# Two forward blocks ahead of the first backward block in the opening of a gated FFT and MLP gradient kernel

## The chip, the cores and the metric

The kernel runs on one core of one Trainium2 chip. The metric is the time of one execution on the device in microseconds (us). Before the change, three runs had a median of 1196.28 us (1195.99 to 1197.32). All other times come from one profiled execution of the same kernel. In its views PE is TensorE, DVE is VectorE, ACT is ScalarE, POOL is GpSimd, and SP is the engine that only issues DMAs. PEld is TensorE's loading of weights. "L783" is line 783 of the kernel.

## What is computed

The reference mixes two branches of one input x with a gate and returns the result and its gradients for a given grad_out. Only the second branch, an MLP, and the gate matter here:

```
g = sigmoid((x * gate_w).sum(-1, keepdims=True))        # one value per row
a = irfft2(rfft2(x) * (w_r + 1j * w_i))                 # branch A
h = relu(x @ w1 + b1) ** 2                              # branch B
b = h @ w2 + b2
out = g * a + (1 - g) * b
# and the gradients of out for x, w_r, w_i, w1, b1, w2, b2, gate_w, given grad_out
```

x has 2048 rows of 1024 values, w1 is 1024 x 3584 and w2 is 3584 x 1024; all are bf16. For the MLP's gradients, the gradient of b is db = (1 - g) * grad_out, and the gradient of the hidden layer is dh = 2 * relu(x @ w1 + b1) * (db @ w2^T).

## The kernel before

**Tiles.** Rows are taken in 16 tiles of 128, the hidden width of 3584 in 28 chunks of 128 (`fc`), and two neighbouring chunks make a pair `fp`. `xT` and `dbT` hold x and db turned (columns on the partitions). A tile is turned by eight TensorE transposes into a PSUM tile `pt` of two buffers (L665, `turn_tile`), which ScalarE or VectorE copies out (L666). `dbn` holds the 16 tiles of grad_out, later scaled by 1 - g (L690, in `gate`).

**The two kinds of block.** A forward step `forth(fp, s, c)` multiplies chunk 2 fp + c of w1 with 512 columns of `xT` (L776, eight matmuls of 128 x 512), takes relu with the bias on ScalarE into `rT` (L777) and, for every second chunk, squares it into `h2T` (L751). A backward step `back_(fp, s, c)` multiplies w2's chunk with 512 columns of `dbT` (L783, eight matmuls), and VectorE turns the PSUM bank `pd` into `dhT` with `rT` (L787). Forward and backward share two PSUM banks (tag `ph`) until the opening ends. `rT` has three buffers, each for both chunks of one (fp, s). `dhT` and `h2T` have two buffers each, every one for 1024 columns of one pair; a full one is stored to DRAM from POOL's queue (L815).

**The opening.** For the first two pairs (fp 0 and 1) the generator `mlp_in` yields after each step, and a loop at the end of the kernel (`for k in range(NT // 4)`) puts the other work between: loads of x and grad_out tiles on SP's queue (L1744, L1748), turning, gate sums, and steps of `first_stage`, the first part of the FFT. For s = 0, 1, 2 the order is four forward steps and four backward steps; for s = 3 the forward steps alone, whose backward steps are left to the first unit of the main part. Work between is put out in the same order: x tiles 4 to 7 are loaded early and turned beside the first backward block.

**Loads.** x tiles live in pairs, in a tag `xsrc` of three buffers that `first_stage` later uses for `u`. A pair's buffer comes free when both tiles are turned and VectorE has taken their gate sums (`gate_of`, L680: one product with gate_w and a sum). w2 comes in groups of 512 columns, turned by the DMA itself (L183, two halves each); group 0 is `w2T` for pairs 0 and 1, group 1 for pairs 2 and 3. The other DMA issues stand in POOL's queue: the four constants `kf`, `flip`, `sel` and `cf` (L1808), the stores of scaled grad_out tiles to `db_scr` (L1822), the stores of `z_scr` (L239) and the later loads `src` of `first_stage` (L697).

**Sums.** After the opening, the main part multiplies matrices in units of seven products instead of eight. It needs sums and differences of quarters of `xT` (`x_sums`, L859, written over `dbn` tiles 0 to 7 for the first half of the columns and 8 to 13 for the second) and of w1 (`w_sums`, L873, written over the buffer that held gate_w). Before, the four sums of w1 stand behind the last forward step and the four of x in the loop's last turn.

**Order.** Each engine runs its own queue in order, and so do the DMA queues; the order is set when the kernel is built. The builder keeps the program's order by priority, but may put an instruction that can go ahead of one that has to wait. `after(ins, earlier, NoSync)` binds an instruction behind another in this order, without a semaphore; without NoSync it also waits. `later["last"]` is the newest L787 instruction, and `later["newest"]` the newest matmul of L776.

The lines of the opening's plan and of its load of w2:

```
halves of w2T group 0: load_w2(0, halves=(0,)) / load_w2(0, halves=(FGW // 2,))      # L962, L964
for s in range(4):                                                                  # L967
    for what in (forth, back_):
...
if s == 2 and what is forth and fp + c == 0: load_w2(1, later["last"])               # L975
```

## Time and profile before

| what | value |
|---|---|
| median of three runs | 1196.28 us |
| the profiled execution | 1203.86 us |
| its span, first to last instruction | 1202.1 us |
| TensorE busy in the span | 1179.5 us |
| VectorE busy | 893.5 us |
| ScalarE busy | 535.8 us |
| mean granted clock of TensorE | 0.999 |
| first matmul of the first unit (pZ, L884) | 85.22 us |

The time is that of the whole execution, the span that of its instructions; 1.8 us lie around it. In a timeline row the first number is the start from the span's beginning, the second the time to the end of the last of the merged instructions, then come engine, line, operation, output and inputs, shapes and count; in brackets stands how long the engine had been idle and what ended that. A row of a windows table gives, for a stretch, its length, each engine's busy time and number of instructions, the granted clock of TensorE (PEclk), the share of the DMA engines and what they moved. In the opening the rows look like this:

```profile
core 0: us, PE busy (x) PEld busy (x) DVE busy (x) ACT busy (x) POOL busy (x), PEclk, DMA share, GB/s
...
13.60:20.10 6.50, 6.13 (x56) 3.73 (x56) 4.71 (x10) 4.58 (x8) 2.72 (x4) 1.00 0.98 246
20.10:25.10 5.00, 4.90 (x39) 2.88 (x39) 3.00 (x7) 3.84 (x5) 0.00 (x0) 1.00 1.22 129
...
53.00:70.00 17.00, 16.83 (x135) 9.91 (x135) 11.96 (x24) 11.24 (x18) 3.51 (x6) 1.00 1.15 144
```

Stretches of a few microseconds can be told apart: from 20.10 to 25.10 TensorE is busy 4.90 of 5.00 us.

### The profile page before, as it was taken

What the parts mean: (1) busy time and instruction counts of PE and PEld (TensorE: products, weight loads), DVE (VectorE), ACT (ScalarE), POOL (GpSimd) and SP (SyncE); (2) the same over time, 40 slices, a digit from 0 to 9 for tenths busy, and PEclk for the clock granted to TensorE, in tenths of its full rate; (3) what the DMA queues carried; (4) which work ended last, traced back from release to release, by engine and by line L of the source; (5) the groups of instructions that cost most, each with busy time, mean ns of one, the idle gap of its engine ahead of it and who ended that gap; (6) DMA issues with size and microseconds to landing.
All of it is one profiled execution on the core that took longest, in us unless ns stands there. A gap on an engine that the chain in (4) does not pass through costs nothing.

```text
span 1202.1 us, 19429 instructions
## 1 busy us (share of the span) xinstructions
PE 1179.5 (98%) x7181; PEld 636.1 (53%) x7275; DVE 893.5 (74%) x1598; ACT 535.8 (45%) x961; POOL 375.9 (31%) x618
## 2 busy tenths in 40 slices
PE   8989999999999999999999999999999999999998
PEld 5555555443333444444446899999544444444444
DVE  5878887689898887776637666666786677986757
ACT  5657888576767783444414556564201010000000
POOL 0224433665666663553322322321001100000000
PEclk9999999999999999999999999999999999999999
DMA  9998585686969888989897999994889999665530
GB/s 242 295 237 244 179 210 185 203 200 192 220 189 212 246 243 174 206 183 220 202 225 141 232 218 249 252 208 151 258 170 251 270 255 280 192 188 153 179 123 36
DMA packets 329464, 249.84 MB, mean 208 GB/s; under 512 B 187912, under 2 KB 287658, under 8 KB 328858
## 3 DMA queue, kind: packets, MB, share of 16 engines
q1 hardware_dynamic: 268352, 112.12, 44.8%
q0 software_dynamic: 35136, 111.72, 29.4%
q10 hardware_dynamic: 25882, 24.76, 7.3%
q8 instruction: 57, 0.93, 0.3%
q14 instruction: 37, 0.30, 0.1%
HBM read 114.82 MB, written 89.67 MB: 170 GB/s over the span
## 4 chain that ended last, share of the span: by engine, by line
PE 73%; DVE 12%; DMA 5%; ACT 4%; issue 4%; SPq 1%; POOL 0%; ACTq 0%; another core or an unknown queue 0%; DVEq 0%; POOLq 0%
PE pX L1206 15%; PE xX L1505 13%; PE pV L1206 11%; PE pd L783 8%; PE xV L1505 6%; PE ph L884 6%; PE xZ L1505 3%; DMA dhT_scr<-dhT 1%; PE pui L325 1%; DVE rT L900 1%; PE ph L776 1%; PE pki L591 1%; PE px L435 1%; DVE dhT L787 1%; DMA z<-z_scr 1%
## 5 line engine op out<-in xcount | busy, mean ns | idle before, releaser
L783 PE MATMUL pd<-dbT,w2T 128*128 128x512 bf16 x859 | 205.4, 379 | 4.4 <-DMA w2T<-in_B_w_dram 2.0
L783 PEld LDWEIGHTS <-w2T 128*128 128x128 bf16 x896 | 86.3, 98 | 106.4 <-issue 3.9
L1505 PEld LDWEIGHTS <-dS 128*128 128x128 f16 x686 | 66.3, 98 | 79.1 <-issue 3.4
L787 DVE SCALAR_TENSOR_TENSOR dhT<-pd,rT 128x512 bf16<-128x512 f32 x112 | 76.6, 684 | 32.7 <-PE pd L783 26.0
L1556 POOL DMA_DIRECT2D out_dram<-ot x32 | 17.3, 542 | 249.4 <-DVE ot L1612 128.0
L1622 ACT ACTIVATE w2br<-w2br,dsc 128x512 f32<-128x512 bf16 x8 | 5.8, 722 | 175.0 <-DVE ot L1612 117.4
L1222 ACT COPY u<-pX 128x512 f32<-128x512 f32 x56 | 32.8, 585 | 98.7 <-PE pX L1206 92.6
L1505 PE MATMUL xX<-oT,dS 128*128 128x512 f16 x336 | 76.5, 379 | 0.2 <-DVE eR L1534 0.2
L1505 PEld LDWEIGHTS <-odd 128*128 128x128 bf16 (+1 forms) x462 | 44.8, 98 | 51.5 <-issue 0.9
L1505 PEld LDWEIGHTS <-even 128*128 128x128 bf16 (+1 forms) x448 | 43.6, 98 | 52.6 <-issue 0.7
L1206 PEld LDWEIGHTS <-T 128*128 128x128 f16 x672 | 64.7, 98 | 7.9 <-issue 0.7
L901 ACT ACTIVATE rT<-rT 128x512 bf16<-128x512 bf16 x69 | 43.3, 628 | 40.7 <-DVE rT L900 40.7
L751 ACT ACTIVATE h2T<-rT 128x1024 bf16<-128x1024 bf16 x56 | 59.7, 1065 | 0.5 <-issue 0.2
L1226 DVE TENSOR_TENSOR whi<-pV,u 128x512 bf16<-128x512 f32 x28 | 19.3, 690 | 51.6 <-ACT u L1222 48.1
L475 POOL DMA_DIRECT2D y_scr<-pc x64 | 46.9, 734 | 34.4 <-DVE pc L472 31.9
L446 DVE TENSOR_TENSOR tt<-x,w 128x1028 f16<-128x1028 f16 (+1 forms) x64 | 41.9, 691 | 17.0 <-issue 12.5
L1206 PEld LDWEIGHTS <-S 128*128 128x128 f16 x336 | 32.3, 98 | 41.0 <-DVE S L1138 1.3
L1206 PEld LDWEIGHTS <-resL 128*128 128x128 bf16 x448 | 43.0, 98 | 4.7
L1206 PEld LDWEIGHTS <-resR 128*128 128x128 f16 (+1 forms) x448 | 42.9, 98 | 4.9 <-issue 0.2
L1206 PEld LDWEIGHTS <-even 128*128 128x128 bf16 (+1 forms) x256 | 24.5, 98 | 30.8 <-issue 2.1
L815 POOL DMA_DIRECT2D h2T_scr<-h2T x28 | 20.7, 738 | 62.1 <-ACT f L285 30.8
L499 POOL DMA_DIRECT2D out_dram<-gw x64 | 34.4, 543 | 17.8 <-ACT gw L495 13.9
(381 smaller groups left out, 2757.8 us busy)
## 6 DMA issues: line engine op xcount, KB each, us to landing
h2T_scr<-h2T POOLq DMA_DIRECT2D x28, 512.0 KB, 4.4
dhT_scr<-dhT POOLq DMA_DIRECT2D x28, 512.0 KB, 5.2
y_scr<-pc POOLq DMA_DIRECT2D x64, 128.0 KB, 3.9
ax_scr<-yo POOLq DMA_DIRECT2D x16, 512.0 KB, 5.4
out_dram<-ot POOLq DMA_DIRECT2D x31, 256.0 KB, 3.1
z<-z_scr ACTq DMA_DIRECT2D x60, 128.0 KB, 4.4
out_dram<-whi POOLq DMA_DIRECT2D x28, 256.0 KB, 5.3
out_dram<-wlo POOLq DMA_DIRECT2D x28, 256.0 KB, 5.2
```

Of the source, the lines that this page charges most:

```text
L446: V(out=tt[:, k, :, :, 0:W], in0=x[:, a : a + 2, :, 0:W], in1=by, op=ALU.mult)
L475: st(out=columns_of(y_scr, c, h), in_=pc[:, n])
L499: st(out=every(dst_w, k), in_=gw[lanes[n], c_, 0:W1])
L751: after(nc.scalar.activation(h2T, rT, ACT.Square), behind_, mybir.DependencyClass.NoSync)
L783: mm(pd[:], lhsT=w_[:, ec, fc % FGC * P : (fc % FGC + 1) * P], rhs=dbT[:, ec, ss], start=(ec == 0), stop=(ec == DC - 1),)
L787: return STT(out=dhT, in0=pd[:], scalar=2.0, in1=rT, op0=ALU.mult, op1=ALU.mult, accum_out=gb1part[:, fc, sb : sb + 1],)
L815: st(out=scr[2 * fp : 2 * fp + 2, :, cols2].rearrange("c p s -> p c s"), in_=t_[:])
L884: mm(acc[:], lhsT=lhs[:, t, :], rhs=rhs[:, t, :], start=start and t == 0, stop=t == KH - 1, skip_group_check=True)
L901: nc.scalar.activation(rT, rT, ACT.Relu)
L1206: self.mm = mm(out, lhsT=lhs[:, t, m * P : (m + 1) * P], rhs=rhs[:, t, :], start=start and t + a == 0, stop=t == KH - 1, skip_group_check= ...
L1222: turn["ACT"] = nc.scalar.copy(out=t_[:], in_=self.X[:])
L1505: ins = mm(acc, lhsT=lhs[:, fc, :], rhs=rhs[:, fc, :], start=start and fc == 0, stop=fc == KH - 1 and bias is None, skip_group_check=True,)
```

## The change

The opening's steps come from one list `plan` of 28: forward blocks 0 and 1 (four steps each), backward 0, forward 2, backward 1, and then, pair by pair, forward 3 and backward 2. Both halves of w2T group 0 are loaded together, after x tiles 4 to 7; group 1 is loaded at step 24 of the plan, behind the backward step before it; w1's third pair at step 16. Three blocks of rows are now between their forward and backward steps, so the `rT` of pair 1, block 1 takes the buffer `cu` of the later units. The four sums of w1 are dealt one each to the steps 24 to 27 (one is taken at a step's end), and three of x's four to the same stretch, the last behind it.

The loop is rewritten for the new order: three turns instead of four, after an opening stretch of its own in which x tiles 4 to 7 are loaded and turned. x 4 and 5 are loaded ahead of the first grad_out tiles. The gate sums of x 4 to 7 go behind the copy of the third turned grad_out tile. The constants are issued in two steps, and the copies of turned x tiles 5 and 7 move from ScalarE to VectorE. The last two pairs of grad_out tiles are turned at the end. Two bindings are new: a turned tile's first transpose goes behind the newest forward matmul, and the scaling of grad_out behind the newest `dhT`.

```diff
@@ -662,7 +662,9 @@
 
         pt = tps.tile([P, DC, P], BF16, name="pt", tag="tr", bufs=2)
         for b in range(DC):
-            nc.tensor.transpose(pt[:, b, :], src[:, b * P : (b + 1) * P], identb[:])
+            one = nc.tensor.transpose(pt[:, b, :], src[:, b * P : (b + 1) * P], identb[:])
+            if b == 0:
+                after(one, later.get("newest"), mybir.DependencyClass.NoSync)
         return copy(out=dst[:, :, of_tile(i)], in_=pt[:])
 
     def vectors(vrow):
@@ -687,7 +689,8 @@
         nc.scalar.activation(omg[:, c_], pg, ACT.Sigmoid, scale=-1.0)
         nc.scalar.activation(gcol[:, c_], pg, ACT.Sigmoid)
         for i in range(i0, i0 + 4):
-            nc.vector.tensor_scalar(out=dbn[:, i, :], in0=dbn[:, i, :], scalar1=omg[:, i : i + 1], scalar2=None, op0=ALU.mult)
+            scaled = nc.vector.tensor_scalar(out=dbn[:, i, :], in0=dbn[:, i, :], scalar1=omg[:, i : i + 1], scalar2=None, op0=ALU.mult)
+            after(scaled, later.get("last"), mybir.DependencyClass.NoSync)
 
     def ahead_to(n, earlier=None):
         for j in range(len(xs), min(n + 1, NT)):
@@ -789,11 +792,10 @@
                 accum_out=gb1part[:, fc, sb : sb + 1],
             )
 
-        def load_w2(fg, earlier=None, halves=(0, FGW // 2)):
-
-            if fg not in w2T:
-                w2T[fg] = wb.tile([P, DC, FGW], BF16, name="w2T", tag="w2T", bufs=2)
-            for h in halves:
+        def load_w2(fg, earlier=None):
+
+            w2T[fg] = wb.tile([P, DC, FGW], BF16, name="w2T", tag="w2T", bufs=2)
+            for h in (0, FGW // 2):
                 f0 = fg * FGW + h
                 after(turned(w2T[fg][:, :, h : h + FGW // 2], B_w2[f0 : f0 + FGW // 2, :]), earlier)
 
@@ -819,7 +821,7 @@
         def forth(fp, s, c, by_rows=False):
             first, at = (s % 2 == 0, s % 2) if by_rows else (c == 0, c)
             if first:
-                pair[0] = new_rT()
+                pair[0] = wb.tile([P, 2, SW], BF16, name="rT", tag="cu", bufs=1) if (fp, s) == (1, 1) else new_rT()
             rT = pair[0][:, at, :]
             hidden(2 * fp + c, rows_(s), w1[fp], rT)
             rTs[fp, s, c] = rT
@@ -959,26 +961,24 @@
         load_w1(1)
         yield
         half_hidden(0, 0), half_hidden(1, 0)
-        load_w2(0, halves=(0,))
         yield
-        load_w2(0, halves=(FGW // 2,))
+        load_w2(0)
         yield
-        waiting = []
-        for s in range(4):
-            for what in (forth, back_):
-                for fp in range(2):
-                    for c in range(2):
-                        if s == 3 and what is back_:
-                            waiting.append((fp, s, c))
-                        else:
-                            what(fp, s, c)
-                        if s == 2 and what is forth and fp + c == 0:
-                            load_w2(1, later["last"])
-                        yield
-            if s == 1:
+        steps = lambda what, s, fps=(0, 1): [(what, fp, s, c) for fp in fps for c in range(2)]
+        plan = steps(forth, 0) + steps(forth, 1) + steps(back_, 0) + steps(forth, 2) + steps(back_, 1)
+        plan += [step for fp in range(2) for step in steps(forth, 3, (fp,)) + steps(back_, 2, (fp,))]
+        for n, (what, *step) in enumerate(plan):
+            what(*step)
+            if n == 16:
                 load_w1(2)
-        for _ in w_sums(2, True):
-            pass
+            elif n == 24:
+                load_w2(1, later["last"])
+                first_sums = w_sums(2, True)
+            if n > 23:
+                next(first_sums)
+            yield
+        waiting = [(fp, 3, c) for fp in range(2) for c in range(2)]
+        next(first_sums, None)
         seq = [(fp, sp) for fp in range(2, LAST - 2) for sp in range(2)]
         seq += [(fp, sp) for sp in range(2) for fp in (LAST - 2, LAST - 1)] + [(LAST, 1)]
         freed = seq.index((LAST - 1, 0))
@@ -1748,13 +1748,13 @@
             ld(out=dbn[:, i, :], in_=go_perm[i])
 
     def turn_x(i):
-        copied = turn_tile(xT, i, rows[i], nc.vector.tensor_copy if i in (1, 3) else nc.scalar.copy)
-        if i > 3:
+        copied = turn_tile(xT, i, rows[i], nc.vector.tensor_copy if i in (1, 3, 5, 7) else nc.scalar.copy)
+        if i > 7:
             gate_of(i, rows.pop(i), later["last"])
         return copied
 
     def turn_grad(i):
-        turn_tile(dbT, i, dbn[:, i, :], nc.scalar.copy if i in (1, 3) else nc.vector.tensor_copy)
+        return turn_tile(dbT, i, dbn[:, i, :], nc.scalar.copy if i in (1, 3) else nc.vector.tensor_copy)
 
 
     zeros = f1.tile([P, H], BF16, name="zeros", tag="zeros")
@@ -1774,9 +1774,14 @@
     vrow = f1.tile([FC + DC, P], BF16, name="vrow", tag="vrow")
     nc.scalar.dma_start(out=vrow[FC : FC + DC, :], in_=gate_w.rearrange("(fc p) -> fc p", p=P))
     nc.scalar.dma_start(out=vrow[0:FC, :], in_=B_b1.rearrange("(fc p) -> fc p", p=P))
+    def constants(*names):
+        for to, name in names:
+            after(st(out=to[:], in_=cten[name].ap()), later["newest"])
+
     next(units)
     rows_of_x(0, 2, 2)
     next(units)
+    rows_of_x(1, 2)
     rows_of_grad(0)
     for i in range(2):
         turn_x(i)
@@ -1788,51 +1793,73 @@
         last_turned = turn_x(i)
     for i in range(4):
         gate_of(i, rows.pop(i), last_turned if i else None)
-    rows_of_x(1)
+    rows_of_x(1, 2, 2)
     next(units)
-    stage = None
-    for k in range(NT // 4):
+    next(units)
+    next(units)
+    gate(0)
+    next(units)
+    turn_x(4), turn_x(5)
+    constants((kf, "kf"), (flip, "flip"), (sel, "sel"))
+    next(units)
+    turn_x(6), turn_x(7)
+    for k in range(3):
         i = 4 * k
-        if k + 1 < NT // 4:
+        if k == 0:
+            rows_of_x(2, 2)
+        if k < 2:
             rows_of_grad(k + 1)
         next(units)
-        if k:
-            turn_grad(i), turn_grad(i + 1)
+        turn_grad(i), turn_grad(i + 1)
         next(units)
-        turn_grad(i + 2) if k else gate(0)
+        turned_ = turn_grad(i + 2)
+        if k == 2:
+            turn_grad(i + 3), gate(12)
+        next(units)
+        if k < 2:
+            turn_grad(i + 3)
+        if k == 0:
+            constants((cf, "cf"))
+            for n in range(4, 8):
+                gate_of(n, rows.pop(n), turned_)
+            rows_of_x(2, 2, 2)
         next(units)
         if k:
-            turn_grad(i + 3)
-        else:
-            for to, name in ((kf, "kf"), (flip, "flip"), (sel, "sel"), (cf, "cf")):
-                after(st(out=to[:], in_=cten[name].ap()), later["newest"])
-            for n in range(4):
-                turn_grad(n)
-        next(units)
-        if stage:
             next(stage)
         next(units)
-        if k + 1 < NT // 4:
-            turn_x(i + 4), turn_x(i + 5)
+        if k < 2:
+            turn_x(i + 8), turn_x(i + 9)
+        else:
+            sums_of_x = later["x_sums"](0)
+            next(sums_of_x)
         next(units)
-        if k + 1 < NT // 4:
-            turn_x(i + 6), turn_x(i + 7)
+        if k < 2:
+            turn_x(i + 10), turn_x(i + 11)
+        else:
+            next(sums_of_x)
         next(units)
-        for n in ((), (0,), (4, 8), (12,))[k]:
-            after(st(out=db_scr[:, n : n + 4, :], in_=dbn[:, n : n + 4, :]), later["last"])
-        if k + 1 < NT // 4:
+        after(st(out=db_scr[:, i : i + 4, :], in_=dbn[:, i : i + 4, :]), later["last"])
+        if k == 2:
+            next(sums_of_x)
+        if k < 2:
             gate(4 * (k + 1))
-        if k + 2 < NT // 4:
-            rows_of_x(k + 2)
+        else:
+            turn_grad(12), turn_grad(13)
         if k == 0:
-            ahead_to(1)
+            rows_of_x(3), ahead_to(1)
             stage = first_stage()
+        elif k == 1:
+            rows_of_grad(3)
         next(stage)
-        if k == 3:
-            for _ in later["x_sums"](0):
-                pass
         next(units)
+        if k == 2:
+            turn_grad(14), turn_grad(15)
         next(stage)
+    after(st(out=db_scr[:, 12:16, :], in_=dbn[:, 12:16, :]), later["last"])
+    next(stage), next(stage)
+    for _ in sums_of_x:
+        pass
+    next(stage)
     V(out=gpg[:], in0=gcol[:], in1=omg[:], op=ALU.mult)
     later["more_banks"]()
 
```

## Prediction before the run

> **What bounds the kernel now.** I read the page first: TensorE is busy 98% of the span, so a change of order can only give back time in which TensorE stands still or runs below its clock. Then I cut the opening into stretches and looked for such time.
>
> ```profile
> PE 1179.5 (98%) x7181; PEld 636.1 (53%) x7275; DVE 893.5 (74%) x1598; ACT 535.8 (45%) x961; POOL 375.9 (31%) x618
> ```
>
> ```profile
> core 0: us, PE busy (x) PEld busy (x) DVE busy (x) ACT busy (x) POOL busy (x), PEclk, DMA share, GB/s
> ...
> 25.10:27.10 2.00, 0.02 (x1) 0.02 (x2) 1.97 (x7) 1.50 (x2) 0.00 (x0) 1.00 0.83 276
> ...
> 70.00:73.45 3.45, 0.00 (x1) 0.01 (x1) 0.76 (x3) 0.75 (x2) 0.00 (x0) 1.00 1.49 221
> 73.45:77.40 3.95, 3.95 (x17) 2.05 (x18) 3.95 (x11) 1.44 (x4) 1.87 (x3) 0.57 0.93 266
> ```
>
> Two holes stand out, and after the second the granted clock is 0.57 for 4 us. TensorE's timeline names what ended each; the chain of waits says where the second comes from.
>
> ```profile
> 27.08 3.63 PE L783 MATMUL pd<-dbT,w2T 128*128 128x512 bf16 x15 [2.00 <-DMA w2T<-in_B_w_dram]
> ...
> 73.45 0.64 PE L776 MATMUL ph<-xT,w1g 128*128 128x512 bf16 x2 [3.46 <-DVE dhT L787]
> 73.89 1.16 PE L325 MATMUL pu<-cf,ft 128*128 128x256 f16 x8
> 74.84 2.68 PE L776 MATMUL ph<-xT,w1g 128*128 128x512 bf16 x6
> ```
>
> ```profile
> 54.69 17.88 DMA dhT_scr<-dhT
> ...
> 72.69 0.71 DVE dhT L787 x2
> ```
>
> The first backward block stops at 25.1 because the second half of w2T has not landed. At 70.0 both PSUM banks are full: VectorE may not write the fourth dhT tile before the store of the second, issued at 54.69, has left it 17.88 us later. SP's queue shows that store's neighbour, the turned load of w2T's second group, issued from 53.26 for 19.59 us; the other stores and loads issued beside it took as long.
>
> ```profile
> 4.18 4.28 SPq L1748 DMA_DIRECT2D dbn<-in_grad_out_dram  x4
> 8.51 5.19 SPq L183 DMA_TRANSPOSE w2T<-in_B_w_dram  x1
> 13.74 2.98 SPq L1744 DMA_DIRECT2D xsrc<-in_A_x_dram  x4
> 16.77 3.12 SPq L183 DMA_TRANSPOSE w2T<-in_B_w_dram  x1
> ...
> 23.97 3.89 SPq L697 DMA_DIRECT2D src<-in_A_x_dram  x3
> 28.25 0.95 SPq L1744 DMA_DIRECT2D xsrc<-in_A_x_dram  x2
> ...
> 53.26 19.59 SPq L183 DMA_TRANSPOSE w2T<-in_B_w_dram  x2
> ```
>
> **What the change takes away.** No matmul, copy or DMA is added or dropped; all terms are waits.
>
> First hole: backward block 0 now comes after eight forward matmul groups of 1.73 us (chain of waits), near 32 us, while w2T's halves are issued at most some 8 us later than now and the second took 10.3 us (16.77 to 27.03): it lands by about 30, and the half that needs it runs near 36. Saved 2.00.
>
> Second hole: the store of dh[1,0] now starts after the second backward block and its tile is next written six groups and four turned tiles later (6 x 1.73 + 4 x 0.45 = 12.2 us). The turned load of w2T group 1 is tied to a backward step after that store. Without it beside them, the dhT store at 47.64 landed in 5.9. Saved 3.45, and with it the slow clock: from 73.45 to 77.36 TensorE does 8 forward matmuls (1.73) and 8 pu matmuls (0.52, from 49.09 to 49.61), 2.25 us of work in 3.91, so 1.66. If the cover is gone and the store is late after all, 5.1 of it comes back. Sum saved: 2.00 + 3.45 + 1.66 = 7.11.
>
> **What it adds.** (a) Forward block 1 needs x tiles 4 to 7 at once. Tiles 6 and 7 go into the slot of tiles 0 and 1, read last by VectorE's gate sum (L680) that ends at 12.84. TensorE reaches them at 13.59 + 1.73 + 0.89 (two turned tiles) + 1.73 = 17.94. SP is free at about 9.4 (8.51 plus two more x loads of 0.43). In the queue of before, src loads that were ready went ahead of x tiles 10 and 11 that still waited for a slot; so I expect w2T's first half (5.19 us) at 9.4 and x 6 and 7 at 14.6 and 15.3. Loads issued there took 4.2 to 5.3 us, so tile 7 lands at 20.6, is turned by 21.05 and copied by 21.8 (0.69), and the forward matmuls start 3.0 after 17.94 + 0.89 = 18.8. The turned tiles that are now bound behind the newest forward matmul (L665) leave nothing to fill this. From below: if x 6 and 7 go first, at 12.9, they land at 18.2 and only the copy is seen, 0.8. From above: behind both halves, tile 7 lands at 24.7 (15.3 + 3.12 + 6.2), the hole is 7.1, and the clock's 1.66 on top: 8.8; but in before they stood ahead of the second half. I take 3.0, the case that the queue's own row supports.
>
> (b) x tiles 10 and 11 wait for gate sums 4 and 5, tied behind dbn tile 2's copy: 27.3 + 2 x 1.27 = 29.9, plus 0.4 for the second issue and 5.4 to land (median of the x loads) = 35.7; TensorE wants tile 11 at about 35.3 (21.8, six groups, six turned tiles and the first half of the pair). 0.5; from 0 (landing in the shortest 3.2) to 2.4 (the longest, 7.4).
>
> (c) VectorE. Between the first dhT and the last sum of w1 it worked 54.05 of 65.8 us (22.06 to 87.86). The gate sums that opened this list now wait until 27.3, and forward block 1 gives it little to do before. To finish 2.9 earlier it needs 54.05 / 57.7 = 0.94 of the time; its densest row is 0.90 (30 to 40), the units run at 0.85 (85.2 to 120). The excess can slide into the first unit, where the last sums are needed some 8 us in and it has 3.2 us free (10.63 of 13.8 busy). I take 0.7 for bank frees that come late; bounds 0 and the 5.7 that the units' share gives (second rival).
>
> (d) The four turned gradient tiles ahead of the last backward pair: two copies of 0.69 in a row on VectorE, up to 1.0, but a forward group of the other weights is ready to run there, as two forward matmuls ran ahead of waiting turned tiles at 15.3. Nothing taken. (e) The copies of x 5 and 7 move from ScalarE (1.01) to VectorE (0.69) in its empty stretch: nothing. (f) The four constants go out in two steps on POOL's queue; the last, cf, took 8.8 and is read some 20 us later: nothing, and each us beyond costs one. (g) rT in the slot of cu: its reader, a backward step near 53, ends 30 us before cu's first copy; nothing. (h) w1's third load: it landed in 7.8 and is read 30 us later. (i) w2T group 1 is issued near 71 and took 21.6 and 18.3 us at worst; its first half is read by the second unit, near 97. Nothing; 10 us of cover. Sums spread over the last eight blocks are the same eight instructions.
>
> Net: 7.11 - 3.0 - 0.5 - 0.7 = 2.9 faster. The profiled execution took 1203.86 (span 1202.1 and 1.8 around it), 7.6 over the median of 1196.28; I subtract from the median: **1193.4**. The later part is as full as now (TensorE 34.1 of 34.8 from 85.2 to 120), so what the opening gains should stay.
>
> **Rivals.** One: the holes close. x 6 and 7 land in time (0.8) and VectorE slides (0, 0): 7.1 - 0.8 = 6.3 faster, 1190.0. For it: before's waits are nearly all these two holes; against: the SP order. [...]
>
> Two, the slower side: VectorE becomes the opening's bound. Place: from 27.3 on, backward blocks 0 to 2. At the units' share the list takes 54.05 / 0.853 = 63.4 and ends at 90.7, 2.8 after now: 1199.1. It decides from a share below 54.05 / (87.86 - 27.3) = 0.89. For it: every gate sum, fold and dhT now lies in 57 us; against: 0.90 was reached in one row and not all must end before the units.
>
> Three: the stall only changes its store. Now w2T's turned load starts near 71, and db_scr of dbn tiles 8 to 11 (1 MB) is issued near 77.3 beside it. The second set of x sums (L859) overwrites these tiles; now it starts 5.7 us into the units (90.89 against 85.2), so near 87.8. A store at 6.2 to 9.9 lands by 87.2; one at 15.7 to 18.9, as beside the load at 53, lands at 93 to 96. VectorE would stand still 5 to 8 us, of which some 3 are covered before TensorE lacks a bank: 2 to 5, say 4. Then 2.9 - 4 = 1.1 slower, 1197.4. Against: beside the next turned load at 102.89 the dhT store took only 8.4.
>
> Four: the w2T wait or the dhT stall remains, as if nothing were moved: 1196 to 1197.
>
> **How the numbers follow.** Forecast 0.41 (its own range 1191.5 to 1195.5), rival one 0.22, two 0.20, three 0.14, four 0.03. 0.2% is 2.4 us, about what can be told from no change. Faster by more: 0.31 of the forecast's share and all of rival one, 0.53. Slower: 0.18 of rival two, 0.06 of three, 0.24. Within: 0.23. The range runs from 1189.2 (all 7.1 saved) to 1200, past rival two; beyond lies the upper bound of (a).
>
> **What would show it.** Right: no 2.00 wait for w2T in the first backward block, no dhT wait on a dhT_scr store, granted clock 1.00 from 70 to 78, a hole of about 3 near 19 to 22 released by an xT copy, the first pZ near 82.3 (85.22 now). Wrong: x 6 and 7 issued behind both halves of w2T; VectorE over 0.92 busy from 27 on with TensorE waiting for dbT or dhT; x sums L859 released by a db_scr store; a hole over 3.45 followed by a clock below 1.

## The result, and the profile after

The changed kernel took 1204.59 us (median of six runs, 1202.78 to 1205.32), the kernel before 1196.34 beside it (six runs, 1195.6 to 1199.31): a ratio of 1.0061, interval 1.0042 to 1.008. It is 8.25 us slower, where 2.9 us faster was forecast. The profiled execution of after took 1204.63 us (span 1202.9, granted clock 0.997), so it is an ordinary one. One profiled execution of before (in before_again, 1532.81 us), with a granted clock near 0.75 throughout, is left out of everything below.

The profile page's line of busy times hardly differs from before's (TensorE 1180.4 us against 1179.5, VectorE 895.4 against 893.5); 0.7% of the span can't be told from it.

TensorE's timeline of after, from the first forward block to the third, has the row that matters:

```profile
20.01 1.90 PE L779 MATMUL ph<-xT,w1g 128*128 128x512 bf16 x7 [0.79 <-ACT xT L668]
...
31.33 1.89 PE L786 MATMUL pd<-dbT,w2T 128*128 128x512 bf16 x8
36.50 0.68 PE L665 MATMUL pt<-identb,xsrc 128*128 128x128 bf16 x8 [3.28 <-DMA xsrc<-in_A_x_dram]
38.29 1.03 PE L665 MATMUL pt<-identb,xsrc 128*128 128x128 bf16 x8 [1.11 <-DMA xsrc<-in_A_x_dram]
39.12 0.63 PE L786 MATMUL pd<-dbT,w2T 128*128 128x512 bf16 x1
39.97 5.06 PE L786 MATMUL pd<-dbT,w2T 128*128 128x512 bf16 x14 [0.22 <-issue]
44.86 1.89 PE L779 MATMUL ph<-xT,w1g 128*128 128x512 bf16 x8
...
71.19 3.63 PE L786 MATMUL pd<-dbT,w2T 128*128 128x512 bf16 x16 [0.94 <-ACT h2T L754]
```

Neither of the two holes forecast to close is there: the first backward block doesn't wait for w2T, and none of these waits is for a `dhT` held by its store. In their place TensorE stands at 33.05 in front of the transposes of x tiles 10 and 11, which have not landed. The backward matmuls behind them in its queue (39.12, 39.97) could have run, as turn_late below shows, but here they stand behind the transposes in the order of the queue.

SP's timeline of after shows what stood ahead of those two tiles:

```profile
13.16 0.81 SPq L1744 DMA_DIRECT2D xsrc<-in_A_x_dram  x2
14.01 5.83 SPq L183 DMA_TRANSPOSE w2T<-in_B_w_dram  x2
19.95 0.99 SPq L1744 DMA_DIRECT2D xsrc<-in_A_x_dram  x2
20.98 1.85 SPq L1748 DMA_DIRECT2D dbn<-in_grad_out_dram  x4
22.88 2.43 SPq L700 DMA_DIRECT2D src<-in_A_x_dram  x4
25.66 1.68 SPq L1748 DMA_DIRECT2D dbn<-in_grad_out_dram  x3
28.18 0.85 SPq L1744 DMA_DIRECT2D xsrc<-in_A_x_dram  x2
```

And the list of DMA issues, for 28.1 to 29.05 us, shows how long they took (median us from issue to landing stands last):

```profile
xsrc<-in_A_x_dram SPq DMA_DIRECT2D x2, 256.0 KB, 9.0
```

Eleven loads of 256 KB (four `dbn`, four `src`, three `dbn`), 2.75 MB, go out in the 7 us before 28.18, with an `h2T` store of 512 KB and `cf` from POOL's queue beside them. The rows of stretches show how busy the DMA engines were (a share of 1.06 and 1.05, with 395 and 365 GB/s moved) and what the wait did to the clock:

```profile
core 0: us, PE busy (x) PEld busy (x) DVE busy (x) ACT busy (x) POOL busy (x), PEclk, DMA share, GB/s
28.70:33.05 4.35, 4.35 (x33) 2.36 (x31) 4.28 (x9) 3.97 (x6) 0.73 (x1) 1.00 1.06 395
33.05:39.10 6.05, 1.67 (x17) 1.26 (x17) 3.31 (x7) 1.01 (x1) 0.00 (x0) 0.82 1.05 365
39.10:44.86 5.76, 5.54 (x18) 2.17 (x17) 2.48 (x8) 1.21 (x3) 0.62 (x1) 0.60 0.85 312
70.00:78.00 8.00, 7.01 (x42) 3.48 (x41) 4.98 (x11) 3.05 (x5) 1.03 (x2) 1.00 0.97 264
```

From 33.05 to 44.86 TensorE turns two tiles (2 x 0.45 = 0.89) and does 16 backward matmuls (16 x 0.216 = 3.46): 4.35 us of work in 11.81. The wait cost 7.46 us: 3.28 + 1.11 of standing still and most of the rest at a low granted clock, 0.82 and 0.60 in the mean of these two rows. Shorter stretches show which wait lowered it:

```profile
36.80:37.20 0.40, 0.38 (x6) 0.14 (x3) 0.40 (x1) 0.00 (x0) 0.00 (x0) 0.65 1.15 355
37.20:37.50 0.30, 0.00 (x0) 0.00 (x0) 0.30 (x1) 0.28 (x1) 0.00 (x0) 0.50 1.15 336
```

The second wait begins at 37.18 (36.50 + 0.68), and by 37.20 the clock is already at 0.50: it fell behind the first wait alone, the one of 3.28 us.

So a new hole explains the size. It does not explain why nothing of the 7.11 us that was to be saved shows. For that, more profiles of before were wanted; they are the first of the experiments.

### The profile page after: what moved, and what is told of

Its sections match the earlier page's. It is cut to its first block, busy times and chain, and to the rows that moved or that the text cites. A ratio compares the mean times of both kernels' runs of the same rounds, so it can differ in the third digit from the quotient of the medians.

```text
span 1202.9 us, 19437 instructions
## 1 busy us (share of the span) xinstructions
PE 1180.4 (98%) x7182; PEld 637.1 (53%) x7275; DVE 895.4 (74%) x1600; ACT 534.1 (44%) x959; POOL 376.7 (31%) x618
## 4 chain that ended last, share of the span: by engine, by line
PE 79%; DVE 11%; ACT 4%; issue 3%; DMA 2%; POOL 1%; ACTq 0%; SPq 0%; DVEq 0%; POOLq 0%
PE pX L1206 15%; PE xX L1505 14%; PE pV L1206 12%; PE pd L786 11%; PE xV L1505 7%; PE ph L886 6%; PE xZ L1505 4%; PE ph L779 2%; PE pui L325 1%; PE pki L591 1%; DVE rT L902 1%; PE px L435 1%; PE pu L325 1%; PE pk L293 1%; PE pv L466 1%
## 5 line engine op out<-in xcount | busy, mean ns | idle before, releaser
L786 PE MATMUL pd<-dbT,w2T 128*128 128x512 bf16 x867 | 208.9, 382 | 3.0 <-ACT h2T L754 0.9
L446 DVE TENSOR_TENSOR tt<-x,w 128x1028 f16<-128x1028 f16 (+1 forms) x64 | 42.0, 691 | 17.9 <-issue 11.9
L410 POOL COPY w<-wn 128x512 bf16<-128x512 bf16 x32 | 21.1, 658 | 64.1 <-DVE tt L446 61.9
```

Of the source, the lines that this page charges most:

```text
L446: V(out=tt[:, k, :, :, 0:W], in0=x[:, a : a + 2, :, 0:W], in1=by, op=ALU.mult)
L786: mm(pd[:], lhsT=w_[:, ec, fc % FGC * P : (fc % FGC + 1) * P], rhs=dbT[:, ec, ss], start=(ec == 0), stop=(ec == DC - 1),)
```

## The experiments

All executions are compared by one stretch of the opening: from the second half of the first forward pair (the row of 16 matmuls of 128 x 256) to the second unit's row of four pZ matmuls. What follows it takes 1099.7 to 1100.0 us in the prediction's profile of before, in after and in gates_early, and 1099.5 to 1100.8 in all others but before_w2_late (1106.1, explained below).

| kernel | stretch, us | its length | median, us (ratio to before, interval) |
|---|---|---|---|
| before, the profile of the prediction | 11.76 to 102.11 | 90.35 | that execution: 1203.86 |
| before_look, before again | 13.77 to 96.78 | 83.01 | that execution: 1198.19 |
| before_third, before again | 11.86 to 94.86 | 83.00 | that execution: 1196.14 |
| before_fourth, before again | 11.33 to 94.34 | 83.01 | that execution: 1196.09 |
| after | 12.00 to 103.21 | 91.21 | 1204.59 (1.0061, 1.0042 to 1.008) |
| gates_early | 11.38 to 95.86 | 84.48 | 1197.58 (1.0006, 0.9996 to 1.0016) |
| loads_behind | 12.17 to 97.39 | 85.22 | 1197.79 (1.0006, 0.9997 to 1.0015) |
| turn_late | 11.39 to 97.25 | 85.86 | 1199.88 (1.0026, 1.0015 to 1.0036) |
| grads_split | 11.78 to 97.11 | 85.33 | 1198.45 (1.0017, 1.0008 to 1.0025) |
| grads_split_fill | 11.46 to 96.48 | 85.02 | 1198.32 (1.0016, 1.0005 to 1.0026) |
| w2_old_place | 11.93 to 96.41 | 84.48 | 1197.69 (1.0008, 0.9998 to 1.0018) |
| turned_ahead | 11.24 to 95.58 | 84.34 | 1197.25 (1.0004, 0.9995 to 1.0013) |
| before_w2_late | 13.76 to 96.78 | 83.02 | 1198.54 (1.0027, 1.0005 to 1.0048) |

The ratios are to runs of before that were taken beside each kernel: their median was 1196.06 (35 runs) for gates_early, loads_behind, before_again and before_w2_late, 1196.53 (27) for turn_late and the two grads_split kernels, and 1197.04 (23) for w2_old_place and turned_ahead. Each stretch is that of one profiled execution.

### Are the two holes in every execution of before?

before_look, before_again, before_third and before_fourth are the kernel before, unchanged.

> The kernel before again, for a profile of an ordinary execution: of its 35 timed runs beside the last set, 30 lie between 1195.1 and 1197.4 and one at 1202.1. Theory A (the two holes belong to rare executions in which a turned load of w2 runs slow): span near 1194.3, no wait for w2T near 25 and no 3.45 us wait for a dhT store near 70, clock 1.00 throughout, the turned load at 53 issued in about 9 us instead of 19.6, and the first unit's second product from w1 (99.21 in the profile of before) at 91 to 92.5, so earlier than in gates_early (92.97). Theory B: both holes are there and the rest of the span is shorter.

> The kernel before, unchanged, for a second look at its own executions. Its profiled execution took 1203.86 us while its timed runs had a median of 1196.3. Theory A (the dhT hole is rare): in another execution the dhT store lands in about 6 to 9 us, TensorE has no 3.45 us hole near 70, the clock stays at 1.00 and the first pZ comes near 80 instead of 85.2; span near 1194.5. Theory B (the hole is in every execution and the profiled one lost time elsewhere): the hole of 3 to 4 us ended by a dhT store is there again, with a clock near 0.6 after it. Time 1196 to 1197 under both.

Eleven executions of before_again had a median of 1196.07 (ratio 1.001, 0.9995 to 1.0025): nine took 1195.32 to 1197.68 and two took 1202.98 and 1203.76. Of the 35 runs of before beside it one was above 1200, at 1202.09. The profile that the prediction was made from, at 1203.86, belongs to that small group.

before_look had neither hole, but its first 16 matmuls of 128 x 256 took 3.56 us (1.92 in the prediction's profile), and its stretch began 2.0 us later. TensorE came to the second half of backward block 0 at 26.93, when w2T could have landed even if it was as late as in the first profile (27.03). The first hole might only have been hidden there. Hence two more:

> The kernel before, unchanged, for one more profile. Theory A: both holes of the prediction's profile (2.00 us in front of the second half of backward block 0, 3.46 us near 70 us with a slow clock behind it, 7.1 in all) belong to rare executions. An execution of 1195 to 1198 us whose stretch starts near 11.8 then has neither, its second half of backward block 0 starts near 25.0 with a wait under 0.5, and the stretch is 82.5 to 83.5 long. Theory B: only the second hole is rare (5.1 us), and the first was missing in the earlier second profile because that one started 2.0 us late; then the wait of about 2 in front of that half is there (27.0), the stretch is near 85.0, and the time of such an execution is near 1198.

> The kernel before, unchanged, once more, so that not all hangs on one execution. Theory A: as for the third profile, a stretch of 82.5 to 83.5 us and neither hole where the time is 1195 to 1198. Theory B: a wait of about 2 us for w2T near 25 to 27 us, a stretch near 85. Either theory allows an execution near 1203, which then has the second hole.

Both began on time, at 11.86 and 11.33, took 1196.14 and 1196.09, and have neither hole. TensorE's timeline of before_third at the places of the two:

```profile
25.01 3.62 PE L783 MATMUL pd<-dbT,w2T 128*128 128x512 bf16 x15
28.95 1.90 PE L776 MATMUL ph<-xT,w1g 128*128 128x512 bf16 x8 [0.32 <-DVE dhT L787]
...
67.87 0.59 PE L776 MATMUL ph<-xT,w1g 128*128 128x512 bf16 x2
...
71.01 1.89 PE L776 MATMUL ph<-xT,w1g 128*128 128x512 bf16 x7
```

No bracket stands on the pd row at 25.01, where TensorE had waited 2.00 us for w2T, and none on the ph rows, where it had waited 3.46. For the second hole, its list of DMA issues from 52 to 60 us says why:

```profile
dhT_scr<-dhT POOLq DMA_DIRECT2D x1, 512.0 KB, 11.5
...
w2T<-in_B_w_dram SPq DMA_TRANSPOSE x2, 12.2
```

The `dhT` store landed 11.5 us after its issue (10.6 in before_fourth) against 17.9 in the first profile, and the turned load of w2T beside it took 13.44 us to issue (12.97) against 19.59. Both are slow each time, but the hole opens only where they are slower still. It isn't a matter of when the load leaves: in before_look it went out at 53.23, as in the first profile (53.26), and took 13.81 us to issue, and the store landed after 11.6. The stretches' rows give the sums: before_third, the profile of the prediction, after.

```profile
11.86:94.86 83.00, 81.31 (x631) 48.16 (x645) 71.34 (x142) 55.78 (x99) 21.54 (x36) 1.00 0.92 277
```

```profile
11.76:102.11 90.35, 83.14 (x632) 48.81 (x646) 71.68 (x142) 55.82 (x99) 21.54 (x36) 0.98 0.99 255
```

```profile
12.00:103.21 91.21, 83.78 (x632) 49.23 (x645) 73.09 (x144) 54.12 (x97) 21.30 (x36) 0.96 0.80 251
```

Set against the second row, after looks 0.9 us slower; set against the first it is 8.21, close to the measured 8.25. Of these, 5.74 are idle time of TensorE (91.21 - 83.78 = 7.43 against 83.00 - 81.31 = 1.69), and 2.47 are the same work at a lower clock (83.78 against 81.31). The split is good to some tenths only, because a few matmuls are missing from the records, not the same number in each profile.

### Is the new hole the whole loss?

gates_early takes the sums that free the buffer of x tiles 10 and 11 ahead of the turned grad_out tiles, so that the two loads go out earlier, with less in front of them:

```diff
-    turn_x(6), turn_x(7)
+    turn_x(6)
+    turned_x = turn_x(7)
+    for n in (4, 5):
+        gate_of(n, rows.pop(n), turned_x)
...
-            for n in range(4, 8):
+            for n in (6, 7):
                 gate_of(n, rows.pop(n), turned_)
```

> The changed kernel with the gate sums of x tiles 4 and 5 bound behind the copy of x tile 7 instead of that of grad_out tile 2, so that the buffer for x tiles 10 and 11 is free some 5 us sooner and their loads stand ahead of the src loads. Theory A (the late x tiles cost 7.5 us: 4.4 idle at 33 to 38 and 2.9 of slow clock after it): the hole at x tiles 10 and 11 is gone, clock 1.00 from 30 to 50, and the time falls by 6 to 8, to 1197 to 1199. Theory B (VectorE is the bound, the hole hides its lag): TensorE waits later for dbT or dhT instead, VectorE over 0.92 busy from 27 on, and the time falls by less than 2, to 1203 or more.

loads_behind leaves the sums and the issue where they are, and puts the loads that aren't wanted yet behind that of x tile 11 in the queue:

```diff
-            ld(out=dbn[:, i, :], in_=go_perm[i])
+            loaded = ld(out=dbn[:, i, :], in_=go_perm[i])
+            if k > 1:
+                after(loaded, x11[0], mybir.DependencyClass.NoSync)
...
+                if j < 2:
+                    after(loaded, x11[0], mybir.DependencyClass.NoSync)
...
+            if fp == 2:
+                after(loaded, x11[0], mybir.DependencyClass.NoSync)
```

(The first cut is on the grad_out tiles from 8 on, the second on the `src` loads, the third on w1's third pair.)

> The changed kernel with the loads of src, of grad_out tiles 8 to 15 and of w1's third pair bound behind the load of x tile 11 on SP's queue; the gate sums stay where they are, so x tiles 10 and 11 are issued at 28 as now, but with little ahead of them. Theory A1 (the tiles are late because some 2.7 MB of less urgent loads share the DMA engines with them): they land 4 to 5 us after issue instead of 9, by 33, the hole shrinks from 4.4 us to under 1 and the clock stays up: 1198 to 1200. Theory A2 (they are late because of the slot, freed at 28): landing stays near 8 and the time near 1204. Theory B (VectorE): as for the run before, 1203 or more, with waits for src or dbT.

Both remove the hole. In TensorE's timelines the 16 transposes of x tiles 10 and 11 now stand in one row with no bracket, in gates_early

```profile
32.44 1.06 PE L665 MATMUL pt<-identb,xsrc 128*128 128x128 bf16 x16
```

and in loads_behind:

```profile
33.23 1.06 PE L665 MATMUL pt<-identb,xsrc 128*128 128x128 bf16 x16
```

SP's timelines and the lists of issues say when the loads left and how long they took. In gates_early they left at 22.63 and landed after 5.5 us; these are the rows of loads_behind (issues of 28 to 29.3 us):

```profile
28.34 0.82 SPq L1750 DMA_DIRECT2D xsrc<-in_A_x_dram  x2
```

```profile
xsrc<-in_A_x_dram SPq DMA_DIRECT2D x2, 256.0 KB, 4.6
```

The same load of the same tiles, issued as late as in after (28.18), lands in 4.6 us instead of 9.0 once the `src` and later `dbn` loads stand behind it: what was queued in front of it set the landing. And 1204.59 falls to 1197.58 or 1197.79, 7.0 and 6.8 us, where 7.46 was read off the timeline. The profiled execution of loads_behind, at 1199.75 the slowest of its twelve, has one new wait of 0.76 us at 95.42, where TensorE waits for ScalarE's `f`. Whether the edit makes it isn't shown.

turn_late leaves the loads of these two tiles as they are and moves their use: x tiles 10 and 11 are turned two backward steps later, and the next `gate` and the loads of x tiles 12 to 15 go with them.

```diff
-        if k < 2:
+        if k == 1:
             turn_x(i + 10), turn_x(i + 11)
...
+        if k == 0:
+            turn_x(10), turn_x(11)
+            gate(4), rows_of_x(3)
```

> The changed kernel with the turning of x tiles 10 and 11 put behind backward block 0 (two backward steps later); their loads, slots and everything ahead of them on the queue stay. Theory A (TensorE stands in its queue behind transposes whose tiles land at 36.4 and 38.2): the two steps fill the hole, some 1.2 us of it and a copy of 1.0 remain, no slow clock: 1198.5 to 1200. Theory B (the loads' bandwidth is the bound, whatever TensorE does first): the hole moves to the next tile that lands late, 1203 or more.

Its median is 1199.88. Two short waits remain, and the clock stays up:

```profile
37.01 0.62 PE L665 MATMUL pt<-identb,xsrc 128*128 128x128 bf16 x8 [0.49 <-DMA xsrc<-in_A_x_dram]
38.73 1.67 PE L779 MATMUL ph<-xT,w1g 128*128 128x512 bf16 x7 [1.10 <-ACT xT L668]
```

```profile
30.00:40.00 10.00, 8.35 (x61) 4.60 (x60) 9.27 (x23) 4.62 (x9) 1.29 (x2) 1.00 1.07 388
```

The median is 2.3 us behind that of gates_early, the stretch 1.38 (the profiled execution, at 1198.97, was the fastest of its ten); the two waits make 1.59. With the backward matmuls ahead of them instead of behind, the late tiles cost far less, though the second lands little sooner: the wait for it ends at 37.01, where it ended at 38.29 in after.

### Can what remains be won?

gates_early still waits in small pieces: 0.79 for the copy of x tiles 6 and 7, 0.42 and 0.30 for copies of turned grad_out tiles, 0.94 ahead of the last backward pair. The row names ScalarE's `h2T` for the last, which ends at 63.83; VectorE's timeline shows the copies of the turned grad_out tiles ending at 63.8 too, where these matmuls start (63.84). The matmuls read `dbT` and not `h2T`, so it is taken to be the copies, and turned_ahead below, where these tiles are turned sooner, bears it out.

```profile
63.84 3.63 PE L786 MATMUL pd<-dbT,w2T 128*128 128x512 bf16 x16 [0.94 <-ACT h2T L754]
```

```profile
62.50 1.29 DVE L668 COPY dbT<-pt 128x1024 bf16<-128x1024 bf16 x2 [0.20 <-PE pt L665]
```

grads_split has the sums of gates_early and gives the odd ones of these copies to ScalarE:

```diff
-        return turn_tile(dbT, i, dbn[:, i, :], nc.scalar.copy if i in (1, 3) else nc.vector.tensor_copy)
+        return turn_tile(dbT, i, dbn[:, i, :], nc.scalar.copy if i % 2 else nc.vector.tensor_copy)
```

> gates_early with every odd turned grad_out tile copied out by ScalarE instead of VectorE (six more of them: 5, 7, 9, 11, 13, 15). In gates_early VectorE copies tiles 10 and 11 one after the other and the backward step that reads them waits 0.94 us, two other turned tiles wait 0.42 and 0.30 for a PSUM buffer. Theory A (these three waits are VectorE's copies): they shrink to about 0.3 in all and the time falls by 1 to 1.4, to 1196.2 to 1196.6. Theory B (ScalarE's queue of relu and copies answers with waits of its own): same time as gates_early within 0.5, or slower.

The median is 1198.45, no better. The waits moved and grew; here are two of TensorE's rows:

```profile
43.35 1.07 PE L293 MATMUL pk<-kf,f 128*128 128x128 f16 x16 [0.90 <-ACT f L285]
...
65.17 3.61 PE L786 MATMUL pd<-dbT,w2T 128*128 128x512 bf16 x16 [1.87 <-ACT dbT L668]
```

A copy of 1.01 us behind ScalarE's other work comes later than one of 0.69 behind VectorE's, and 0.94 became 1.87.

grads_split_fill adds work to fill the other waits: the copy of x tile 6 goes to VectorE, and grad_out tile 0 is turned ahead of forward block 1.

```diff
-... nc.vector.tensor_copy if i in (1, 3, 5, 7) else nc.scalar.copy)
+... nc.vector.tensor_copy if i in (1, 3, 5, 6, 7) else nc.scalar.copy)
...
+        if k == 0:
+            turn_grad(0)
         next(units)
-        turn_grad(i), turn_grad(i + 1)
+        if k:
+            turn_grad(i)
+        turn_grad(i + 1)
```

> grads_split, and turned grad_out tile 0 ahead of the second forward block, x tile 6 copied by VectorE, so that something fills the 0.79 us in which TensorE waits for the copies of x tiles 6 and 7. Theory A: 0.3 to 0.5 us less than grads_split, near 1196; level with the kernel before, not faster, since that has hardly any hole in an ordinary execution. Theory B: the turned tile waits for a PSUM buffer and nothing is gained.

The median is 1198.32: the first wait fell from 0.79 to 0.34 us, the median by less than can be told.

turned_ahead is gates_early with these two and without the split, and turns grad_out tiles 8 to 11 one forward step earlier, with their scaling (`gate(12)`) later:

```diff
+        elif k == 2:
+            turn_grad(8), turn_grad(9)
         next(units)
...
+        else:
+            turn_grad(10), turn_grad(11)
...
+        if k == 2:
+            gate(12)
```

> gates_early with grad_out tiles 8 to 11 turned one forward step earlier, the scaling of tiles 12 to 15 put behind the third backward block's first half, and tile 0 turned ahead of forward block 1 (x tile 6 copied by VectorE). Theory A (the forward-first order loses 0.94 and 0.79 us to copies that nothing covers, and has nothing else to lose or win against an ordinary execution of the kernel before): both waits go to 0.4 or less, the stretch from the second half of the first forward pair to the second unit falls from 84.5 to about 83.2, against 83.0 in before_look; time 1196 to 1196.6, level with before. Theory B (VectorE's total is the bound): the waits move to other copies, 1197.3 or more.

The median is 1197.25, level with before and with gates_early. The 0.94 is gone, but three other waits stand in its place. These are TensorE's rows, and then the stretch from 70 to 80 us in turned_ahead and in gates_early:

```profile
74.97 1.02 PE L886 MATMUL ph<-xT,w1f 128*128 128x512 bf16 x4 [0.24 <-DVE dhT L790]
76.67 0.38 PE L886 MATMUL ph<-dbn,Sw 128*128 128x512 f16 x1 [0.67 <-ACT cu L890]
...
84.65 0.81 PE L786 MATMUL pd<-dbT,w2T 128*128 128x512 bf16 x3 [0.31 <-DVE rT L902]
```

```profile
70.00:80.00 10.00, 9.03 (x81) 5.58 (x81) 10.00 (x20) 4.92 (x12) 1.84 (x3) 1.00 1.07 314
```

```profile
70.00:80.00 10.00, 9.70 (x85) 5.94 (x84) 10.00 (x20) 4.95 (x12) 1.84 (x3) 1.00 1.13 255
```

VectorE is busy 10.00 of 10 us in both, so it has no time left in either. That this makes the new waits is likely, since two of the three are for its results, but it isn't shown. The whole stretch of the table is only 0.14 us shorter than gates_early's.

### Does the place of w2T's second group matter?

w2_old_place is gates_early with that load at step 12 of the plan instead of 24:

```diff
+            if n == 12:
+                load_w2(1, later["last"])
...
-            elif n == 24:
-                load_w2(1, later["last"])
```

> gates_early with one part of the change undone: the turned load of w2T group 1 goes out at the start of forward block 2, as in the kernel before, instead of behind backward step 23. Theory A (its place decides only how often a slow turned load catches a dhT store): the median is that of gates_early within 0.7 us, 1197 to 1198.3, but some executions lie 4 to 8 us higher, as in the kernel before (5 of 46); gates_early had none in 11. Theory B (the new place is worth time in every execution): 2 us or more slower than gates_early in the median.

The median is 1197.69, with one of twelve executions at 1202.01, and the same stretch to the hundredth (84.48). In this profile the load, at 42.06, took 9.71 us to issue and held nothing up. Moving it later earned nothing in gates_early's order, in the executions seen.

before_w2_late is before with the load moved seven steps later, behind the third backward block, and nothing else:

```diff
-                        if s == 2 and what is forth and fp + c == 0:
+                        if s == 2 and what is back_ and fp + c == 2:
                             load_w2(1, later["last"])
```

> The kernel before with one thing moved: the turned load of w2T group 1 behind the third backward block instead of inside the third forward block, so that it no longer runs beside the dhT store that the hole at 70 waited for. Theory A (the hole is rare): the time is that of before within 1 us, 1195.5 to 1197.5. Theory B (the hole is in every execution): 3 to 5 us faster, 1191 to 1193.

Its median is 1198.54, of eleven runs between 1195.49 and 1210.01, five of them above 1200, a wider spread than before's own. The profiled one has no hole in the opening, but one of 3.81 us further on:

```profile
136.44 1.02 PE L884 MATMUL ph<-xT,w1g 128*128 128x512 bf16 x4 [3.81 <-ACT rT L898]
```

```profile
71.47 15.83 SPq L183 DMA_TRANSPOSE w2T<-in_B_w_dram  x2
...
97.56 22.08 SPq L183 DMA_TRANSPOSE w2T<-in_B_w_dram  x2
```

```profile
105.01 11.04 DMA h2T_scr<-h2T
...
116.34 17.84 DMA src<-in_grad_out_dram
```

The second fence is SP's timeline, the third the chain of waits: beside the turned load of the third group, issued for 22.08 us, a store took 11.04 and a `src` load 17.84, and the granted clock from 130 to 140 was 0.87. So the slow execution is not tied to one place in the opening: in both profiles of this kind a turned load was slow, at 53 us in one and at 97 in the other. Why the load is slow in some executions was not found.

## Why the prediction was wrong

**The term saved, 7.11.** It measured nothing. The two holes and the slow clock behind them were read rightly as far as that profile goes, and after has none of them. But the profiled execution was 7.6 us above the median, and the holes with their clock are 7.11: before's three later profiles have neither, and the stretch is 7.35 us shorter in them (83.00 against 90.35). The prediction put both numbers side by side ("7.6 over the median of 1196.28; I subtract from the median") and did not see that the one is the other. **This step gave the wrong sign**: a gain of one rare execution was taken from the time of all. With its own costs of 4.2 and no gain the same sum would have said 1200.5.

**(b) x tiles 10 and 11, 0.5 (0 to 2.4).** It measured 7.46, and is nearly all of the loss: 7.0 us come back with the hole in gates_early. The issue was not late; the sums ran from 25.62, so it came at 28.18, ahead of the forecast (about 30). TensorE came to tile 11 sooner too (33.05 + 0.45 = 33.5, against 35.3), so these two all but cancel. What failed is the landing: "5.4 to land (median of the x loads)", at the longest 7.4. These are times of loads that had other work ahead of them in the queue. The change puts 2.75 MB of loads into the 7 us in front of these two, and they took 9.0; with less in front, in loads_behind, 4.6. The upper bound also left out the clock, which was priced for (a) alone.

With these two set right, and (a) as measured below, the sum is 1196.28 + 0.79 + 7.46 + 0.7 = 1205.2, against 1204.59; (d), which measured 0.94, is not in it, nor are the small waits of before's own order.

**(a) x tiles 6 and 7, 3.0 (0.8 to 8.8).** The lower bound held: SP stood waiting and issued them at 13.16, ahead of both halves of w2T, and only the copy's 0.79 is seen. That `src` loads had overtaken waiting x tiles elsewhere did not carry over to this place.

**(c) VectorE, 0.7.** Small, as forecast: after has one wait of 0.30 us for its copies, gates_early two, of 0.42 and 0.30. VectorE is full in places (9.27 of 10 us in turn_late's row, 10.00 in those of gates_early and turned_ahead), and rival two's mechanism may show there, at tenths of a microsecond. It was no bound of the opening in after: from 70 to 78 us it is busy 4.98 of 8.

**(d) four turned tiles, nothing.** It measured 0.94: the last backward pair waited, and no forward group ran in that gap.

**(e) to (i), nothing.** None shows as a wait in after's timeline. w2T's second group, issued at 75.58, took 5.54, and its user did not wait.

**Rivals.** One would have needed the gain to exist. Three did not come: no VectorE instruction waits for a `db_scr` store. Four's times (1196 to 1197) come near those of gates_early, though for another reason: not that a hole stays, but that before ordinarily has none. The slower side was sought in VectorE and in stores, and it lay in a load that (b) had already named.

**What was to show it.** The granted clock of 1.00 from 70 to 78 and the vanished waits came as forecast, the first pZ did not: 87.06 against 82.3. The sign that did show is nearly the last of those named: a hole over 3.45 and a clock below 1 behind it; the hole that came was one of 3.28, with 0.60 behind it.

What stays open is how much slower than before gates_early is. The interval of its ratio (0.9996 to 1.0016) holds no change, but its stretch (84.48, and the same in w2_old_place) is 1.47 us longer than those of before's three ordinary profiles, and its median lies 1.52 above that of the runs of before beside it. No version tried beats before; gates_early, loads_behind, w2_old_place and turned_ahead can't be told from it by their ratios.

## What to carry to other kernels

Set the profiled execution beside the median before any hole in it is counted as a gain: where it lies above by as much as the holes are worth, they are likely its own (here 7.6 us above, and holes of 7.11), and a second profile settles it. A load's landing is priced by what the change puts ahead of it in the queue (here 9.0 us with the `src` and later `dbn` loads in front, 4.6 with them behind), not by the median of other loads (5.4); and work that TensorE can do should stand ahead of the instruction that waits for a load, not behind it (1199.88 us in turn_late, 1204.59 in after).

## What the hardware showed beyond that

A turned load of 1 MB of w2T in two halves took 5.5 us to issue in after, 9.7 in w2_old_place, 13.0 to 13.8 in three ordinary profiles of before, 15.8 and 22.1 (groups 1 and 2) in one execution of before_w2_late, and 19.6 in the profile of the prediction. Beside the slowest two, 22.1 and 19.6, an `h2T` store landed after 11.04 us and a `src` load after 17.84, and a `dhT` store after 17.9 and two `src` loads after 18.3 (median). In after the two halves of 512 KB landed 6.4 and 5.4 us after their issue; two plain stores of 1 MB (`db_scr`, in the prediction's profile from 73.4 to 75) landed after 6.2 (median).

Behind one stop of 3.28 us the granted clock halved (1.00 to 0.50), and it fell only after work had begun again: in after some 0.4 us after the transposes started at 36.50 (1.00 from 36.80 to 36.90, 0.59 to 37.00, 0.50 from 37.20). So it did in the prediction's profile, behind 3.46 us of standing still: 0.4 us after the end of the wait at 73.45 (1.00 to 73.85, 0.56 from there to 74.20, then 0.50). There it stayed low for about 3.4 us (0.74 from 77.20 to 77.40, then 1.00), in after for 6.8 (0.57 from 43.40 to 43.80, then 1.00); a second wait fell into that time, but why it was twice as long isn't shown. In before_w2_late (3.81 idle, to 136.44) the clock was 0.87 from 130 to 140 and 0.96 from 140 to 150. If it was 0.50 while it was low, as in the other two, it fell 1.0 us after the end of the wait and stayed low for 3.4, an estimate from these two rows. The 2.00 in the prediction's profile and the 0.49 and 1.10 of turn_late left it at 1.00 (27.10 to 31.00 there, 30 to 50 here).

In after the lost clock cost 2.47 us by the rows of the whole opening, or 2.86 by those of the hole (1.67 + 5.54 us busy for 4.35 of work). That comes on top of the 4.39 of standing still and is more than half as much again.
